# First token tiles turned one by one, W1 units begun on half of them, gate weights loaded as rows, and engine orders written out as a table

## The chip, the cores and the metric

The kernel runs on one core of one Trainium2 chip. A core has a matrix engine (PE), a vector engine (DVE), a scalar or activation engine (ACT), a general engine (POOL), a sequencer that mostly issues transfers (SP), and 16 DMA engines that all queues share. The engines run on their own instruction lists and meet at semaphores. The metric is the time of one execution in microseconds (us), and a version is judged by the median of several runs. The kernel before takes 154.9 us (three runs, 154.64 to 155.01).

## The reference

Two branches read the same 2048 tokens of width 512 and are mixed by a gate per token.

```
g = sigmoid((x * gate_w).sum(-1))                       # one number per token
# branch A: linear attention, 32 heads of 16
q, k, v = split(x @ wqkv)                               # 512 -> 3*512
pq, pk  = q @ w_phi, k @ w_phi                          # per head, 16x16
phi_q = concat(softmax(pq), softmax(-pq)); phi_k the same # 32 features a head
kv = phi_k^T v ; z = sum over tokens of phi_k
a  = ((phi_q kv) / (phi_q z + 1e-6)) @ wo
# branch B: dense layer with ReLU
b  = relu(x @ w1) @ w2                                  # 512 -> 1376 -> 512
out = g * a + (1 - g) * b                               # bf16
```

## The kernel before, in words

Tokens are cut into 16 tiles of 128, and into 4 chunks of 512 for the dense branch. The program is a graph of named tasks: each is one instruction, or a run of matmuls, with an engine, the tasks it depends on, and an assumed length and landing delay. A planner (`schedule`, lines 95 to 121) places the tasks with these assumed lengths, shakes its priorities 200 times, and keeps the order of each engine that gives its shortest plan. `emit` (line 133) then writes every engine's instructions in that order, with a semaphore wait wherever a dependency crosses engines. On the chip each engine follows its list strictly: an instruction that waits holds up all that stand behind it.

The names that the prediction uses:

- `x0a`, `x0b`: the first 512 tokens, loaded as two pieces of two tiles (256 KB each), one on SP's queue and one on ACT's. `xt..` turns them with PE against an identity (line 343; the identity is DVE's `ident`), four 128-column matmuls a bank, and `xe..` moves them from PSUM to `XT` (ACT line 355, DVE line 358). `x1`, `x2`, `x3` are the other three chunks, turned by DMA from SP (line 278); `x1` waits for `w1b1`.
- `w1a`, `w1b0`, `w1b1`, `w1c`: columns 0 to 255, 256 to 767 and 768 on of W1. `gw` puts the 512 gate weights as one more column into W1, element by element. `wka`, `wkb`: the K weights; `wv`: the V weights; `wphi`: the 16x16 head matrices, made block-diagonal by DVE (`wbd`).
- `h{c}_{k}` (line 398): unit k of W1 on chunk c, four matmuls of 512 columns, followed by `rl` (ReLU on ACT, line 413). Unit 10 carries the gate's column too: `gr` clips it, `g1`, `g2` take it through DRAM into one number per partition, `ge`, `gp`, `go` make the gate factors.
- `wt`, `we` (lines 329, 334, 336): K weights turned by PE and moved out. `f1_j`, `fe1_j` (line 373): W_phi folded into them, so that `pr_k..` gives pk directly. `f0_j` does the same for Q, turned by DMA (`wqT`).
- `pr_` (line 469): projections, two tiles a job (one in the last two jobs of a kind). `ev_` (ACT) copies them out, `mx_`, `mn_` (DVE) find the extremes of each head, `t1_`, `t2_` (POOL, line 510) subtract them, `ex_` (ACT) is the exponential, `sm_`, `rc_` (DVE) sum and invert, `nm_` (POOL) scales.
- `v{m}`, `ve{m}` (line 449): values of tile m. `kv{m}` (line 533) accumulates kv and z. `tq` turns phi_q by DMA, `nd{m}_{half}` (line 576) multiplies by kv, `rd`, `o` (DVE) divide, `to` turns the result by DMA.
- `b{m}` (line 597): W2 on tile m, eleven matmuls into one of three banks; `a{m}` (line 603) adds WO's product to the same bank; `oe{m}` (ACT, line 648) empties it; `st{m}` stores. The next user of a bank is `b{m+3}`.
- `warm` (line 260): eight matmuls on zeros while the first loads fly.

The order of the loads on each queue is fixed by hand:

```
load("x0a", "sp", ...); load("x0b", "act", ...); load("w1a", "sp", ...); load("wka", "act", ...)
load("wkb", "sp", ...); load("w1b0", "act", ...); load("w1b1", "sp", ...); load("wv", "act", ...)
load("w1c", "sp", ...); load("wphi", "pool", ...); load("gw", "pool", ...)
```

Of the kernel before, what the change touches and what calls it, by code (L numbers as in the profile page):

```python
# [6 lines left out]
ACT = mybir.ActivationFunctionType  # L7
# [6 lines left out]
ENGINES = ("sp", "pool", "act", "dve", "pe")  # L14

# [20 lines left out]
class _Graph:  # L36
# [28 lines left out]
    @staticmethod  # L65
    def lag(d, u):
        return 0.0 if u in d.behind or d.eng == u.eng == "pe" else d.lat

    @staticmethod
    def place(tasks, before, after, lag, key):  # L70

        left = {t: len(before[t]) for t in tasks}
        ready = {e: [] for e in ENGINES}
        for t in tasks:
            if not left[t]:
                ready[t.eng].append((0.0, t))
        free = dict.fromkeys(ENGINES, 0.0)
        order = {e: [] for e in ENGINES}
        start, end = {}, {}
        for _ in tasks:  # L80
            at, e = min((max(free[e], min(r for r, _ in ready[e])), e) for e in ENGINES if ready[e])
            pick = max((x for x in ready[e] if x[0] <= at), key=lambda x: key[x[1]])
            ready[e].remove(pick)
            t = pick[1]
            order[e].append(t)
            start[t], end[t] = at, at + t.dur
            free[e] = end[t]
            for u in after[t]:
                left[u] -= 1
                if not left[u]:  # L90
                    ready[u.eng].append((max(end[d] + lag(d, u) for d in before[u]), u))
        return order, start, end, max(end[t] + t.lat for t in tasks)

    def schedule(self, rounds=24, shakes=200):


        tasks = list(self.tasks.values())
        before = {t: list(dict.fromkeys(t.deps + t.ahead)) for t in tasks}
        after = {t: [] for t in tasks}
        for t in tasks:  # L100
            for d in before[t]:
                after[d].append(t)
        key = {}
        for t in reversed(tasks):
            key[t] = t.dur + t.lat + max((key[u] for u in after[t]), default=0.0)
        for t in tasks:
            key[t] += t.boost
        best = None
        rng = random.Random(1)
        for n in range(1 + shakes):  # L110
            if n:
                much = rng.choice((0.5, 1.0, 2.0, 4.0))
                at, wide = (rng.uniform(0.0, best[0]), rng.uniform(5.0, 40.0)) if n % 3 else (0.0, 1e9)
                key = {t: k + (much * rng.random() if abs(best[3][t] - at) < wide else 0.0) for t, k in best[2].items()}
            for _ in range(rounds if n == 0 else 3):
                order, start, end, span = self.place(tasks, before, after, self.lag, key)
                if best is None or span < best[0] + (1e-9 if n else -1e-9):
                    best = (span, order, key, start)
                key = {t: end[t] + t.lat for t in tasks}
                _, _, back, _ = self.place(tasks[::-1], after, before, lambda u, d: self.lag(d, u), key)  # L120
                key = {t: back[t] + 0.02 * t.boost for t in tasks}
        return best[1]
# [27 lines left out]
def bass_gated_mix__linear_kernel_hedgehog__dense_activation_relu__prompt_kernel(  # L150
# [33 lines left out]
    NWARM = 8  # L184
    RL = 400.0
    FE = "dve"
    SP0 = -1

    with ExitStack() as es:
# [35 lines left out]
        ROWM = sb("ROWM", [P, GH], I32)  # L225
        GB = sb("GB", [P, P], FP32)
# [55 lines left out]
        def chunk(c):  # L282
            return slice(c * 512, (c + 1) * 512)

        w1r = B_w1.rearrange("(j p) n -> p j n", p=P)
        x0r = x2[chunk(0), :].rearrange("(m p) d -> p m d", p=P)
        wkr = A_wqkv[:, D:2 * D].rearrange("(j p) n -> p j n", p=P)
        load("x0a", "sp", XN[:, 0:2, :], x0r[:, 0:2, :], dur=0.5, lat=3.7)
        load("x0b", "act", XN[:, 2:4, :], x0r[:, 2:4, :], dur=0.5, lat=3.7)
        load("w1a", "sp", W1[:, :, 0:256], w1r[:, :, 0:256], dur=0.5, lat=5.5)  # L290
        load("wka", "act", WK[:, 0:2, :], wkr[:, 0:2, :], dur=0.5, lat=5.0)
        load("wkb", "sp", WK[:, 2:4, :], wkr[:, 2:4, :], dur=0.5, lat=5.8)
        load("w1b0", "act", W1[:, 0:2, 256:768], w1r[:, 0:2, 256:768], dur=0.5, lat=8.0)
        load("w1b1", "sp", W1[:, 2:4, 256:768], w1r[:, 2:4, 256:768], dur=0.5, lat=8.0)
        load("wv", "act", WV[:, :, :], A_wqkv[:, 2 * D:3 * D].rearrange("(j p) n -> p j n", p=P), dur=0.5, lat=11.1)
        load("w1c", "sp", W1[:, :, 768:DFF], w1r[:, :, 768:DFF], dur=0.5, lat=10.4)
        load("wphi", "pool", WPS[:, :, :], A_w_phi.rearrange("(g hl) r c -> (hl r) g c", g=ND), dur=0.9, lat=5.7)
        load("gw", "pool", W1[:, :, DFF:DFF + 1], gate_w.rearrange("(j p o) -> p j o", p=P, o=1), dur=0.8, lat=8.0,
             allow_slow_non_contiguous=True)
        g.follow("iota_r", "iota_i")  # L300
        g.follow("iota_i", "wphi")
        load_t("x1", XT[:, :, chunk(1)], x2[chunk(1), :], ("w1b1",), 2.6, 2.3)
# [35 lines left out]
        XB, WB, FB = (0, 1, 6, 7), (2, 6, 7, 0), (1, 2, 6, 7)  # L338

        def pe_xt(q, p, hf):  # L340
            for n in range(4):
                j, m = 2 * p + n // 2, 2 * hf + n % 2
                last = q.matmul(PS[:, XB[2 * hf + p], n * P:(n + 1) * P], XN[:, m, j * P:(j + 1) * P], IDN[:, :],  # L343
                                start=True, stop=True)
            return last

        for hf, ld in enumerate(("x0a", "x0b")):
            half = slice(hf * 256, (hf + 1) * 256)
            for p in range(2):
                add(f"xt{p}{hf}", "pe", lambda q, p=p, hf=hf: pe_xt(q, p, hf), (ld, "ident"), dur=0.32,  # L350
                    boost=9000.0 - 10 * (ND * hf + p))
                o3 = XT[:, 2 * p:2 * p + 2, half]
                i3 = PS[:, XB[2 * hf + p], :].rearrange("p (j t) -> p j t", j=2)
                if p == 0:
                    add(f"xe{p}{hf}", "act", lambda q, o=o3, i=i3: q.activation(o, i, ACT.Copy), (f"xt{p}{hf}",),  # L355
                        dur=0.6, boost=9000.0)
                else:
                    add(f"xe{p}{hf}", "dve", lambda q, o=o3, i=i3: q.tensor_copy(o, i), (f"xt{p}{hf}",), dur=0.69,  # L358
                        boost=9000.0)
        for i in range(ND):  # L360
            add(f"wt{i}", "pe", lambda q, i=i: pe_turn(q, WB[i], [WK[:, j, i * P:(i + 1) * P] for j in range(ND)]),
                ("wka", "wkb", "ident",
                *((f"xe{XB.index(WB[i]) % 2}{XB.index(WB[i]) // 2}",) if WB[i] in XB else ())), dur=0.28, boost=1900.0)
            evict(f"we{i}", ("act", "dve")[i % 2], WT[:, ND + i, :], WB[i], (f"wt{i}",), boost=1900.0)
        x0 = [f"xe{p}{hf}" for p in range(2) for hf in range(2)]
# [11 lines left out]
        for j in range(ND):  # L377
            b = FB[j]
            war = ["xe10"] if j == 0 else [f"we{j - 1}"]
            add(f"f1_{j}", "pe", lambda q, j=j, b=b: pe_fold(q, 1, j, b), (*wkt, *wbd, *war), dur=0.24,  # L380
                boost=1800.0)
            evict(f"fe1_{j}", ("dve", "act")[j % 2], WP[:, 1, j, :], b, (f"f1_{j}",), boost=1800.0)
# [9 lines left out]
        freed = {b: () for b in HB}  # L392
        w1of = {k: (("w1a",) if k < 2 else ("w1b0", "w1b1") if k < 6 else ("w1c",)) for k in range(KT)}
# [7 lines left out]

        prev = None
        for n, (kind, a, k) in enumerate(units):
            b = HB[n % len(HB)]
            if kind == "h":
                rows = P if k < KT - 1 else KREM
                deps = [*xof[a], *w1of[k], prev, *freed[b]]
                if k == KT - 1:
                    deps.append("gw")
                add(f"h{a}_{k}", "pe", lambda q, a=a, k=k, b=b: pe_h(q, a, k, b), deps, dur=0.87,  # L410
                    boost=8000.0 if n < 2 else 0.0)
# [41 lines left out]
        for m in range(NT):  # L453
            def add(*a, boost=20.0 * (len(widths) * 2 - m // 2 - VLAG), **how):
                return g.add(*a, boost=boost, **how)

            add(f"v{m}", "pe", lambda q, m=m: pe_v(q, m), (*xof[m // 4], "wv", f"ve{m - 1}" if m else "fe1_1"), dur=0.87)
            add(f"ve{m}", "act", lambda q, m=m: q.activation(  # L458
                ap(VS, NT * NG * GZ, m * NG * GZ, [[GZ, NG], [1, GV]]), psap(2 * 512, [[GV, NG], [1, GV]]), ACT.Copy),
                (f"v{m}",), dur=0.6)  # L460
# [14 lines left out]
        for jn, (kind, tiles) in enumerate(jobs):  # L475
# [15 lines left out]
            def old(x, J2=two):  # L491
# [4 lines left out]
                 *([f"ev_{before}"] if before else ["fe1_0", "we3"])], dur=0.87 * w)  # L496
# [16 lines left out]
            if jn == NF - 2:  # L513
                war += [f"xt{p}{hf}" for p in range(2) for hf in range(2)]
# [197 lines left out]
```

## Time and profile before

| what | value |
|---|---|
| median of three runs | 154.9 us |
| the profiled execution | 155.05 us |
| its span in the profile | 153.5 us |
| PE busy | 148.2 us (97%) |
| POOL, DVE, ACT busy | 111.1, 114.2, 93.8 us |
| HBM read, written | 4.94 MB, 2.11 MB |
| first product of real data (line 398) | starts at 7.22 us |
| last product of PE | ends at 150.70 us |

The span runs from the first to the last instruction of the profiled execution; some 1.5 us of its time lie outside. Positions in the text, such as "at 7.22", are us from the start of the span. The chain of waits lists, in order of time, the pieces of work that led to the end, each with its start and its length. In the list of instructions a matmul's length includes its way through the array, so that the step from one to the next is shorter than its length.

### The profile page before, as it was taken

What the parts mean: (1) busy time and instruction counts of PE and PEld (TensorE: products, weight loads), DVE (VectorE), ACT (ScalarE), POOL (GpSimd) and SP (SyncE); (2) the same over time, 40 slices, a digit from 0 to 9 for tenths busy, and PEclk for the clock granted to TensorE, in tenths of its full rate; (3) what the DMA queues carried; (4) which work ended last, traced back from release to release, by engine and by line L of the source; (5) the groups of instructions that cost most, each with busy time, mean ns of one, the idle gap of its engine ahead of it and who ended that gap; (6) DMA issues with size and microseconds to landing.
All of it is one profiled execution on the core that took longest, in us unless ns stands there. A gap on an engine that the chain in (4) does not pass through costs nothing.

```text
span 153.5 us, 2500 instructions
## 1 busy us (share of the span) xinstructions
PE 148.2 (97%) x951; PEld 75.0 (49%) x951; DVE 114.2 (74%) x169; ACT 93.8 (61%) x127; POOL 111.1 (72%) x73
## 2 busy tenths in 40 slices
PE   6799999999999999999999999999999999999992
PEld 2565444554545544545454455444544444455471
DVE  3443668999986999489959969989889797773401
ACT  2366689869598959699789725586083612610331
POOL 7000396999999999999999999999895549260000
PEclk9999999999999999999999999999999999999999
DMA  4999999501000000000000050755869358696421
GB/s 139 261 351 240 134 221 334 156 1 1 6 0 0 0 5 0 2 0 0 1 4 0 10 127 7 138 127 138 193 162 169 102 137 205 152 145 154 117 86 36
DMA packets 43715, 15.59 MB, mean 102 GB/s; under 512 B 36548, under 2 KB 43700, under 8 KB 43704
## 3 DMA queue, kind: packets, MB, share of 16 engines
q1 hardware_dynamic: 39992, 12.08, 37.0%
q10 hardware_dynamic: 3648, 3.34, 6.7%
q0 software_dynamic: 64, 0.02, 0.5%
q8 instruction: 7, 0.11, 0.4%
q14 instruction: 4, 0.03, 0.1%
HBM read 4.94 MB, written 2.11 MB: 46 GB/s over the span
## 4 chain that ended last, share of the span: by engine, by line
PE 96%; DVE 1%; ACT 0%; issue 0%
PE PS L398 25%; PE PS L597 23%; PE PS L469 18%; PE PS L449 9%; PE PS L603 8%; PE PS L533 3%; PE PS L576 3%; PE PS L260 2%; PE PS L618 2%; PE PS L373 1%; PE PS L343 1%; PE PS L329 1%; PE PS L629 1%; DVE XT L358 0%; ACT OSB L648 0%
## 5 line engine op out<-in xcount | busy, mean ns | idle before, releaser
L519 DVE TENSOR_REDUCE ZB<-FT 128x128 f32<-128x2048 bf16 (+1 forms) x18 | 36.6, 2040 | 8.8 <-ACT FT L517 8.8
L398 PE MATMUL PS<-XT,W 128*128 128x512 bf16 (+1 forms) x176 | 41.4, 380 | 0.9 <-DVE XT L358 0.8
L510 POOL TENSOR_TENSOR TS<-MN,PB 128x1024 bf16<-128x1024 bf16 (+1 forms) x18 | 31.1, 1725 | 15.3 <-DVE MN L503 15.3
L597 PE MATMUL PS<-W,HT 128*128 128x512 bf16 (+1 forms) x165 | 38.1, 380 | 0.3 <-ACT OSB L648 0.3
L517 ACT ACTIVATE FT<-TS 128x2048 bf16<-128x2048 bf16 (+1 forms) x18 | 30.9, 1720 | 7.8 <-POOL TS L510 7.1
L510 POOL TENSOR_TENSOR TS<-PB,MX 128x1024 bf16<-128x1024 bf16 (+1 forms) x18 | 30.9, 1722 | 1.9 <-DVE MX L501 1.9
L469 PE MATMUL PS<-WP,XT 128*128 128x512 bf16 x128 | 30.6, 379 | 0.0
L526 POOL TENSOR_TENSOR FT<-FT,SC 128x2048 bf16<-128x2048 bf16 (+1 forms) x9 | 29.6, 3289 | 0.0
L413 ACT ACTIVATE HT<-PS 128x512 bf16<-128x512 f32 (+1 forms) x44 | 25.7, 598 | 6.0 <-PE PS L398 5.9
L398 PEld LDWEIGHTS PS<-XT,W 128*128 128x128 bf16 (+1 forms) x176 | 17.1, 100 | 19.8 <-ACT XT L355 1.0
L648 ACT ACTIVATE OSB<-PS,OMG 128x512 bf16<-128x512 f32 x15 | 10.3, 687 | 26.6 <-PE PS L603 26.1
L597 PEld LDWEIGHTS PS<-W,HT 128*128 128x128 bf16 (+1 forms) x165 | 15.4, 98 | 17.3 <-ACT OSB L648 0.4
L503 DVE TENSOR_REDUCE MN<-PB 128x64 bf16<-128x1024 bf16 (+1 forms) x18 | 19.3, 1074 | 3.5 <-ACT PB L497 3.4
L497 ACT ACTIVATE PB<-PS 128x1024 bf16<-128x1024 f32 (+1 forms) x18 | 16.7, 927 | 8.4 <-PE PS L469 8.1
L501 DVE TENSOR_REDUCE MX<-PB 128x64 bf16<-128x1024 bf16 (+1 forms) x18 | 19.4, 1077 | 2.2 <-ACT PB L497 2.2
L469 PEld LDWEIGHTS PS<-WP,XT 128*128 128x128 bf16 x128 | 12.1, 98 | 13.7
L449 PE MATMUL PS<-WV,XT 128*128 128x512 bf16 x64 | 16.4, 380 | 0.0
L549 POOL TENSOR_TENSOR FT<-FT,SR 128x1024 bf16<-128x1024 bf16 (+1 forms) x9 | 15.6, 1738 | 0.5
L603 PE MATMUL PS<-WO,OT 128*128 128x512 bf16 x60 | 15.1, 379 | 0.0
L584 DVE SCALAR_TENSOR_TENSOR OTM<-PS,EG,RD 128x256 bf16<-128x256 f32 x32 | 13.7, 466 | 0.0
L582 DVE RECIPROCAL RD<-PS 128x16 f32<-128x16 f32 x32 | 6.4, 229 | 7.2 <-PE PS L576 7.2
L458 ACT ACTIVATE VS<-PS 128x512 bf16<-128x512 f32 x16 | 9.5, 597 | 1.9 <-PE PS L449 1.9
(53 smaller groups left out, 96.5 us busy)
## 6 DMA issues: line engine op xcount, KB each, us to landing
out_dram<-OSB ACTq DMA_DIRECT2D x15, 128.0 KB, 1.9
W<-in_B_w_dram SPq DMA_DIRECT2D x1, 1280.0 KB, 7.5
W<-in_B_w_dram SPq DMA_DIRECT2D x1, 608.0 KB, 10.1
W<-in_B_w_dram SPq DMA_DIRECT2D x2, 256.0 KB, 6.4
WV<-in_A_wqkv_dram ACTq DMA_DIRECT2D x1, 512.0 KB, 10.7
WO<-in_A_wo_dram SPq DMA_DIRECT2D x1, 512.0 KB, 7.6
FT<-in_A_x_dram SPq DMA_DIRECT2D x1, 256.0 KB, 3.2
FT<-in_A_x_dram ACTq DMA_DIRECT2D x1, 256.0 KB, 3.5
```

What stands on the lines that cost most here:

```text
L398: last = q.matmul(PS[0:m, b, :], W1[:, j, k * P:k * P + m], XT[:, j, chunk(c)], start=(j == 0), stop=(j == ND - 1))
L413: add(f"rl{a}_{k}", "act", lambda q, a=a, k=k, b=b, rows=rows: q.activation(HT[0:rows, k, chunk(a)], PS[0:rows, b, :], ACT.Relu), (prev,), ...
L449: last = q.matmul(PS[:, 2, :], XT[:, j, m * P:(m + 1) * P], WV[:, j, :], start=(j == 0), stop=(j == ND - 1))
L469: last = q.matmul(PS[:, n, :], XT[:, j, m * P:(m + 1) * P], WP[:, s, j, :], start=(j == 0), stop=(j == ND - 1))
L501: add(f"mx_{J}", "dve", lambda q, sl=sl, w=w, i=pbg: q.tensor_reduce(MX[:, sl, 0:w * H], i, AX.X, ALU.max), (f"ev_{J}", old("t1")), dur=0. ...
L503: add(f"mn_{J}", "dve", lambda q, sl=sl, w=w, i=pbg: q.tensor_reduce(MN[:, sl, 0:w * H], i, AX.X, ALU.min), (f"ev_{J}", old("t2")), dur=0. ...
L510: add(f"{tn}_{J}", "pool", lambda q, o3=o3, a3=a3, b3=b3: q.tensor_tensor(o3, a3, b3, ALU.subtract), (f"{'mx' if sg == 0 else 'mn'}_{J}", ...
L517: add(f"ex_{J}", "act", lambda q, fs=fs, ts=ts, w=w: q.activation(FT[:, fs, 0:w * F], TS[:, ts, 0:w * F], ACT.Exp), (f"t1_{J}", f"t2_{J}", ...
L519: add(f"sm_{J}", "dve", lambda q, fs=fs, sl=sl, w=w: q.tensor_reduce(ZB[:, sl, 0:2 * w * H], FT[:, fs, 0:w * F].rearrange("p (g d) -> p g ...
L526: add(f"nm_{J}", "pool", lambda q, f3=f3, sl=sl, w=w: q.tensor_tensor(f3, f3, SC[:, sl, 0:2 * w * H].unsqueeze(2).to_broadcast([P, 2 * w * ...
L597: last = q.matmul(PS[:, ab, :], HT[0:r, k, m * P:(m + 1) * P], W2[0:r, k, :], start=(k == 0), stop=False)
L603: last = q.matmul(PS[:, ab, :], OT[:, m % NOT, t, :], WO[:, t, :], start=False, stop=(t == ND - 1))
```

## The change

What it does, part by part:

- The first 512 tokens come as four loads `x00` to `x03` of one tile each, two on SP's queue and two on ACT's. Each tile is turned on its own (`xt0` to `xt3`) into two half-filled banks, and moved out by two instructions of 256 columns, one on ACT (`xe{m}0`), one on DVE (`xe{m}1`).
- Units 0 and 1 of W1 on chunk 0 are split: `hh0`, `hh1` use the first 256 tokens, `h0_0`, `h0_1` the other 256.
- The loads are ordered anew: W1's first two column ranges in halves on both queues, then K weights as one load on SP, `w1c` on ACT behind `xe30`, V weights on SP. `x1` waits for `w1c` instead of `w1b1`.
- The gate weights are loaded as four rows of 128 (`GWR`), turned by one small matmul (`gt`) and copied into W1's extra column by DVE (`gv`).
- Four warm matmuls instead of eight; other PSUM banks at the start; Q's fold (`f0`) allowed after the whole of chunk 2.
- The planner is gone. The order of every engine is a written table.

```
-    def schedule(self, rounds=24, shakes=200):
...
+    def schedule(self):
+        order = {e: [self.tasks[n] for n in ORDER[e].split()] for e in ENGINES}
...
+ORDER = {
+    "sp": (
+        "x00 x01 w1a0 w1b0 wk wv x1 x2 g1_0 wqT x3 g2_0 g1_1 g2_1 w2a w2b tq0 wo tq1 g1_2 g1_3 g2_2 to0 tq2 tq3 "
...
+    "pool": (
+        "iota_c iota_r iota_i wphi gw t1_k0 t2_k0 t1_k1 t2_k1 ones nm_k0 t1_k3 t2_k3 t1_k2 t2_k2 t2_k4 t1_k4 "
+        "nm_k1 nm_k2 t2_k6 t2_k5 t1_k5 nm_k3 t1_k6 nm_k4 t2_k7 t1_k8 t1_k7 t2_k8 t2_q0 nm_k5 t1_q0 nm_k6 t1_q1 "
+        "ra_q0 t2_q1 nm_q0 nm_k7 nm_k8 t2_q2 t1_q2 ra_q1 nm_q1 t2_q3 t1_q3 ra_q2 nm_q2 t2_q4 t1_q4 ra_q3 nm_q3 "
...
+    "act": (
+        "x02 x03 w1a1 w1b1 xe00 xe10 xe20 xe30 w1c rl0_0 rl0_1 rl0_2 we2 we0 fe1_1 fe1_3 rl0_4 rl0_3 ev_k0 rl0_6 "
...
+        "rl3_5 ve14 ex_q1 rl3_7 ve15 ev_q4 rl3_6 rl3_8 rl3_9 ev_q5 ex_q2 ge2 oe0 gp2 st0 ex_q3 ev_q6 ge3 oe1 "
+        "ev_q7 ex_q4 oe2 oe3 ex_q5 ev_q8 st1 oe4 oe5 ex_q6 st3 st2 oe7 ex_q7 st5 st4 oe6 st7 oe9 ex_q8 st9 st6 "
+        "oe8 gp3 st8 oe10 oe11 oe12 st12 st10 oe13 oe14 st11 st14 st13 oe15_0 st15_0 "
+    ),
+    "dve": (
+        "zero ident shift xe01 xe11 xe21 blk xe31 wbd3 wbd0 wbd1 wbd2 we3 we1 gv fe1_0 fe1_2 mx_k0 mn_k0 mx_k1 "
+        "mn_k1 sm_k0 rc_k0 gr0 mx_k3 mx_k2 gr1 mn_k3 mx_k4 mn_k2 mn_k4 sm_k1 rc_k1 sm_k2 rc_k2 mn_k5 gr2 mn_k6 "
...
+    "pe": (
+        "warm xt0 xt1 xt2 xt3 hh0 hh1 h0_0 h0_1 h0_2 h0_3 wt3 wt2 wt1 wt0 h0_4 gt f1_0 f1_1 f1_2 f1_3 h0_5 pr_k0 "
+        "h0_6 h0_7 pr_k1 h0_8 v0 h0_9 pr_k2 h0_10 v1 pr_k3 h1_10 v2 h1_0 pr_k4 kv0 kv1 h1_1 h1_2 h1_3 v3 h1_4 "
...
+        "v11 h3_2 h3_3 pr_q2 kv10 v12 kv11 h3_4 h3_5 pr_q3 h3_6 kv12 v13 h3_7 kv13 v14 pr_q4 h3_8 v15 b0 kv14 "
+        "kv15 pr_q5 nd0_0 nd0_1 h3_9 nd1_0 nd1_1 b1 pr_q6 a0 b2 nd2_0 nd2_1 b3 nd3_1 a1 pr_q7 nd3_0 b4 nd4_1 "
+        "nd5_0 nd4_0 pr_q8 a2 nd5_1 a3 b5 nd7_0 nd6_0 nd6_1 b6 a4 nd7_1 a5 b7 nd8_1 nd8_0 b8 a7 a6 nd9_0 nd9_1 "
+        "b10 nd10_1 nd10_0 nd11_0 b9 a9 a8 nd11_1 b12 nd12_0 nd12_1 nd13_0 b11 nd14_1 nd14_0 a10 nd13_1 a11 b13 "
+        "nd15_1 nd15_0 a12 b14 a13 a14 b15 a15_0 a15_1 "
...
-    NWARM = 8
+    NWARM = 4
-    SP0 = -1
+    SP0 = -2
...
+        for n, lat in enumerate((2.7, 3.0, 3.4, 3.3)):
+            load(f"x0{n}", qs[n // 2], XN[:, n, :], x0r[:, n, :], dur=0.5, lat=lat)
+        for name, c0, c1, lat in (("w1a", 0, 256, 3.6), ("w1b", 256, 768, 4.6)):
+            for n in range(2):
+                load(f"{name}{n}", qs[n], W1[:, 2 * n:2 * n + 2, c0:c1], w1r[:, 2 * n:2 * n + 2, c0:c1], dur=0.5, lat=lat)
+        load("wk", "sp", WK, wkr, dur=0.5, lat=5.6)
+        load("w1c", "act", W1[:, :, 768:DFF], w1r[:, :, 768:DFF], dur=0.5, lat=3.2)
+        load("wv", "sp", WV[:, :, :], wvr, dur=0.5, lat=8.3)
+        load("wphi", "pool", WPS[:, :, :], A_w_phi.rearrange("(g hl) r c -> (hl r) g c", g=ND), dur=0.9, lat=6.2)
+        load("gw", "pool", GWR[0:ND, :], gate_w.rearrange("(j p) -> j p", p=P), dur=0.8, lat=4.5)
-        load_t("x1", XT[:, :, chunk(1)], x2[chunk(1), :], ("w1b1",), 2.6, 2.3)
+        load_t("x1", XT[:, :, chunk(1)], x2[chunk(1), :], ("w1c",), 2.6, 2.3)
...
+        def pe_xt(q, m):
+            for j in range(ND):
+                last = q.matmul(PS[:, XB[m][j // 2], (j % 2) * P:(j % 2 + 1) * P], XN[:, m, j * P:(j + 1) * P],
+                                IDN[:, :], start=True, stop=True)
+            return last
+        for m in range(4):
+            add(f"xt{m}", "pe", lambda q, m=m: pe_xt(q, m),
+                (f"x0{m}", "ident", *(("xe00", "xe01") if m == 3 else ())), dur=0.4, boost=9000.0 - 10 * m)
...
+        g.follow("xe30", "w1c")
+        add("gt", "pe", lambda q: q.matmul(PS[:, 2, 0:ND], GWR[0:ND, :], IDN[0:ND, 0:ND], start=True, stop=True),
+            ("gw", "ident", "xe20"), dur=0.06, boost=1500.0)
+        add("gv", "dve", lambda q: q.tensor_copy(
+            ap(W1, ND * W1C, DFF, [[W1C, ND], [1, 1]]), psap(2 * 512, [[1, ND], [1, 1]])), ("gt",), dur=0.15, boost=1500.0)
...
+        def pe_h_half(q, k, b):
+            for j in range(ND):
+                last = q.matmul(PS[:, b, 0:256], W1[:, j, k * P:(k + 1) * P], XT[:, j, 0:256],
+                                start=(j == 0), stop=(j == ND - 1))
+            return last
+        for k in range(2):
+            add(f"hh{k}", "pe", lambda q, k=k: pe_h_half(q, k, HB[k]), (*x0[0:4], "w1a0", "w1a1", prev), dur=0.44, boost=8500.0)
```

## The prediction

> **What bounds the kernel now.** I read the page's first part, then the chain of waits in order of time, then the loads, then busy time by stretch.
>
> ```profile
> span 153.5 us, 2500 instructions
> PE 148.2 (97%) x951; PEld 75.0 (49%) x951; DVE 114.2 (74%) x169; ACT 93.8 (61%) x127; POOL 111.1 (72%) x73
> ```
>
> PE is the bound; a change that leaves its work as it is can only remove idle PE time. The chain shows where that is:
>
> ```profile
> 1.19 3.60 PE PS L260 x8
> 4.79 1.61 PE PS L343 x16
> 6.40 0.02 issue
> 6.43 0.70 DVE XT L358
> 7.13 0.09 issue
> 7.22 1.89 PE PS L398 x8
> 9.11 0.89 PE PS L329 x16
> 10.00 0.10 issue
> 10.09 1.02 PE PS L398 x4
> 11.12 0.89 PE PS L373 x16
> 12.01 1.73 PE PS L398 x8
> 13.74 1.73 PE PS L469 x8
> ...
> 99.81 0.88 PE PS L603 x4
> 100.69 0.02 issue
> 100.71 0.70 ACT OSB L648
> 101.40 0.05 issue
> 101.45 2.55 PE PS L597 x11
> ```
>
> Product work starts at 7.22. From 13.74 to the last matmul at 150.70 PE stops once: 0.77 us (0.02 + 0.70 + 0.05) at 100.69, where b3 needs the bank that a0 has just filled and waits for oe0 to empty it. So two prizes: the start, and 0.77 us. What holds the start is loads and pace:
>
> ```profile
> q0 software_dynamic: 64, 0.02, 0.5%
> DMA to landing us min/median/max: 5.2/7.5/10.1
> 2.00:6.50 4.50, 4.39 (x23) 2.50 (x21) 1.13 (x4) 2.10 (x3) 1.94 (x4) 1.00 1.02 313
> 6.50:7.75 1.25, 0.53 (x3) 0.32 (x4) 1.09 (x4) 0.27 (x1) 0.00 (x0) 1.00 0.80 95
> 7.75:12.00 4.25, 4.16 (x44) 2.77 (x42) 1.89 (x6) 3.02 (x6) 0.00 (x0) 1.00 1.07 348
> ```
>
> The first line is POOL's queue (W_phi and the gate weights): 0.5% of 16 engines' span is 12.3 engine-us for 18 KB. The second is landing time of loads into W tiles within the first 13 us; the shortest, w1a, is issued at 1.26 and lands at 6.47. The last three are stretches (length, then busy time and count of PE, PEld, DVE, ACT, POOL, then clock, DMA share, GB/s): between 6.5 and 7.75 the rate falls from 313 to 95 GB/s while the DMA engines stay 80% busy, which is when the gate weights, 512 scattered elements, move (issued 2.31, 6.6 us to landing).
>
> **The change part by part.** The profiled execution took 155.05 us: 153.5 of span and 1.55 around it. The median of the three runs is 154.9, so sums made from the profile are lowered by 0.15.
>
> *Work.* Matmuls: the same products. hh0, hh1 and the rests of h0_0, h0_1 are 16 of 256 columns for 8 of 512; the 20 of L618 with 256 columns step at 0.11 us (22 in 2.41), half of 0.216, so nothing is added. gt is one tiny matmul (0.06). Four warm matmuls of 0.43 go; they lay before the first data.
>
> *First tokens.* Four 128 KB loads, issued as now at 0.74 and 0.5 us later on each queue. All 512 KB land as now at 4.25 (x0b: 0.75 + 3.5). x00 should land near 3.2: half of x0a's 256 KB left out at 313/2 GB/s is 0.8 off its 0.74 + 3.2; ends 2.9 and 3.94. xt0, 4 matmuls at the cold step of 0.107, is done by 3.9. ACT is not ready: its table load (2.88, 1.28 long) follows its fourth load, as it does in the changed order, so xe00 starts at 4.2; a half eviction costs near the 0.47 of the last tile's halves (0.60 is the 512-column one). xe00 ends at 4.67, and xt3, which reuses its bank, runs 4.75 to 5.2. xe10 ends by 5.1.
>
> *First units.* hh0 needs those and w1a, now two 128 KB pieces with 768 KB moved in all instead of the 1 MB that went by before 6.47: 256 KB at 313 GB/s is 0.84 less, 5.6; counted on from x0b, 4.25 + 0.84 = 5.1. I take 5.4, hh0 at 5.45; ends 5.2 (PE free) and 6.5 (w1a no earlier than now). PE's pace: L343 steps at 0.107 and L329, the same shape, at 0.056; the step changes at about 6.15, 4.95 us after the first matmul (the clock column says 1.00 throughout and does not show it). hh0 to h0_1, 1.73 at full pace, lose half of 0.70: they end at 7.53.
>
> *W1's next columns and the gate weights.* w1b now goes ahead of wk: 1.31 MB instead of 1.83 MB before it is complete. It landed at 9.96 (2.30 + 7.66); 0.5 MB at 348 GB/s is 1.5 less, and the dip, 1.25 x (1 - 95/313) = 0.87, goes with the 2-byte elements (four rows of 256 B). 7.6 at most; from x0b's 4.25 on, 0.79 MB at 348 GB/s give 6.5; PE wants it at 7.53 for h0_2. No wait taken, 0.1 possible. h0_3 ends at 9.26.
>
> *wk.* SP's fifth load, now beside w1c, which ACT issues only after xe30 (about 5.8, moving from 6.8). Near 6.6 all of wk is left; half of 348 GB/s gives 512 KB in 2.8 us: 9.4. Ends 8.7 (w1c late) and 12.1 (the whole first batch, WV's 2.35 + 10.7, less 0.87). wt starts at 9.45, h0_4 and all after it queued behind.
>
> *To the first projection.* wt 0.89, h0_4 0.86, gt 0.06; f1 waits for we1 (wt3's eviction starts at 9.87, two DVE casts of 0.69: 11.16, which h0_4 covers to 11.2): 11.26 to 12.15. h0_5 to 13.01; fe1_2, second of two casts from 11.68, ends at 12.98: pr_k0 at 13.08. Now it starts at 13.74 with one unit fewer done, so like for like at 14.60: **gain 1.52**.
>
> *Queues moved past.* SP issues x1's transpose after w1c (about 11.5, now 9.97): landings go from 14.9 to 16.8 and, for x2, from 18.9 to 21; pr_k2 wants x1 at 20.8, pr_k4 x2 at 28.6. g1_0 stands ahead of wqT and x3 and waits for gr0 near 27: x3 lands at about 35.5, pr_k6 wants it near 44, w2 near 86. All covered, by 4 us or more. On POOL iota_c ahead puts W_phi 0.2 later; it landed at 7.2, and wbd is wanted at 11.2. ones (0.69) moves from 3.26 to behind t2_k1, where POOL ends it at 25.5, before rc_k0 at 26.25.
>
> *The written-out order.* b2 (2.38) and nd2 (0.26) now stand between a0 and b3, against the 0.94 that b3 needed (nd2, right behind a0, starts at 100.51, b3 at 101.45): **0.77 gone**. What is tight next: b4, b5, b7, b12 and b13 have one a (b4: a one-tile pr) and one nd, 0.99, between filling and reuse; ACT must take the eviction within 0.05. Also kv0 (nm_k0: POOL from 26.3, 3.68 long, ends at 29.98; PE is there at 30.3) and kv15 right behind nm_k8. I charge 0.30 for these; ends 0 and 0.77, one stall like today's.
>
> Sum: 155.05 - 1.52 - 0.77 + 0.30 = 153.06, less 0.15: **152.9**.
>
> **The rivals.**
>
> *The pace doubles later.* Today PE runs without a gap from 1.19 until it doubles; then it has gaps near 3.0 and 3.7 us, some 0.6 in all. If the 4.95 us must be unbroken they start again at hh0 and end at 10.4: 2.48 lost, the four half units end at 11.38, pr_k0 starts at 15.01, 0.41 later than like for like: 155.05 + 0.41 - 0.77 + 0.30 - 0.15 = 154.84, no change. For it: fewer warm matmuls. Against it: PE is still busy four fifths of the 3 us before 6.15 (four xt of 0.43, 0.70 of hh0). The Trainium skill, TensorE: Matmul & The Clock Gate, Part 1, says full pace comes after one busy window of about 3.4 us of a free-running monitor; a missed window would by that be made good 3.4 us after 6.15, for which I estimate 154.4. The trace allows that rule (4.95 us from a cold start hold one whole window), but what share of a window must be busy neither says.
>
> *wk lands last.* PE's order is fixed, so everything stands behind wt. If wk is served after w1c and wv (12.1), wt starts at 12.15, pr_k0 at 15.78, 1.18 late: **155.6**, slower. It decides from a landing at 11.9. For: wk gains a competitor on the other queue, and lands now at 8.4 with less ahead of it. Against: wv is behind wk on the same queue.
>
> *The transfers hide the split.* w1a's last piece lands at 6.47 as now, hh0 at 6.52, already at full pace: pr_k0 at 13.61, gain 0.99, **153.4**.
>
> **How the numbers follow.** Forecast 0.60 (own range 152.3 to 153.4: wt near 8.9, or 0.77 of new waits), hidden split 0.15, late pace 0.14, late wk 0.11. A measurement tells 0.3%, 0.46 us, from no change. Faster: the first two, 0.75. Same: 0.14. Slower: 0.11. The range runs from 152.3 to 154.9 (late pace); late wk is left out.
>
> **What would show it.** The first W1 unit near 5.45 instead of 7.22; L329's successor near 9.45; the first WP product near 13.1; no 95 GB/s stretch; the idle time before b3 gone and less than 0.3 us of PE waits after 16 us. It is wrong if the first 128-column steps are still 0.107 after 7 us, if wt waits beyond 10, or if PE waits for ACT at several of the b's named.

## The result, and the profile after

The changed kernel takes 159.87 us (median of six runs, 158.68 to 162.32) against 154.85 for the kernel before (six runs, 154.64 to 155.3). The ratio is 1.0308, 95% interval 1.0238 to 1.0377: slower by 3%, where 152.9 was forecast. A ratio here leaves out runs more than 1.5% above the fastest of the same kernel, which a median and a range do not.

The profiled execution took 160.96 us with a span of 158.8; 153.5 was the span before. The six times lie in two groups, three from 158.68 to 158.9 and three from 160.84 on, and the profiled one is of the longer group. From its page, in the same order as before (the clock row has 40 slices of 4 us):

```profile
span 158.8 us, 2511 instructions
...
PE 150.1 (95%) x956; PEld 75.6 (48%) x956; DVE 121.1 (76%) x172; ACT 93.2 (59%) x129; POOL 111.0 (70%) x73
...
PEclk9999999999999999999997799999999999999999
...
q0 software_dynamic: 64, 0.02, 0.1%
```

DVE has 6.9 us more of busy time than before, though it has only three more instructions. The granted clock dips once, in the middle. The gate weights no longer hold the DMA engines: POOL's queue is down from 0.5% to 0.1%. The chain of waits, in order of time, shows the three places that matter:

```profile
1.68 5.58 DMA W<-in_B_w_dram
7.26 0.14 issue
7.40 1.87 PE PS L408 x8
9.27 1.53 PE PS L414 x8
10.79 1.73 PE PS L402 x8
12.52 0.89 PE PS L330 x16
13.41 0.86 PE PS L402 x4
14.28 0.11 PE PS L365
14.38 1.00 PE PS L377 x16
15.38 0.86 PE PS L402 x4
16.24 1.84 PE PS L495 x8
...
70.72 5.40 DVE MK L319
76.12 2.20 DVE ZB L545
78.32 2.25 DVE MX L527 x2
80.57 0.87 DVE SC L549
81.44 0.07 issue
81.51 3.68 POOL FT L552
85.19 0.05 issue
85.24 0.43 PE PS L559 x8
...
103.75 0.86 PE PS L629 x4
104.62 2.38 PE PS L623 x11
106.99 0.26 PE PS L602 x8
107.25 2.38 PE PS L623 x11
```

- Start: `hh0` begins at 7.40, not 5.45, because a piece of w1a lands at 7.26. The first WP product starts at 16.24; like for like, before had 14.60. That is 1.64 lost.
- Middle: the chain leaves PE for a DVE instruction of 5.40 us, line 319. It is `mk`, which makes a mask of 128x4 numbers. Behind it on DVE stand the sum, the extremes and `rc_k6`, and `nm_k6` on POOL waits for that; `kv12` on PE waits for `nm_k6`.
- End: behind `a0` (103.75) come `b2`, `nd2` and, at 107.25, `b3`, each at once. The 0.77 us stall is gone.

PE's two longest waits (us in total, times, longest), and then three stretches of 3.41 us (length, busy time and count of PE, PEld, DVE, ACT, POOL, granted clock, DMA share, GB/s):

```profile
PE PS L559 <- POOL FT L552: 2.7, 1, 2.7
PE PS L408 <- DMA W<-in_B_w_dram: 1.9, 1, 1.9
```

```profile
7.06:10.48 3.42, 3.08 (x15) 2.24 (x16) 0.77 (x4) 0.32 (x1) 0.00 (x0) 1.00 1.09 382
...
82.16:85.57 3.41, 0.71 (x11) 0.34 (x10) 3.41 (x5) 3.10 (x4) 3.41 (x2) 1.00 0.00 0
85.57:88.98 3.41, 3.41 (x14) 1.22 (x12) 3.41 (x6) 1.09 (x2) 2.50 (x3) 0.50 0.00 0
```

The wait for `nm_k6` costs 2.70. It leaves PE busy for only 0.71 of 3.41 us, and in the next 3.41 us the granted clock is 0.50: PE works all the time at half pace and loses another 1.71. The span's difference comes out: 1.64 + 2.70 + 1.71 - 0.77 = 5.28, against 158.8 - 153.5 = 5.3. Outside the span lie 2.2 us instead of 1.55, which no view of the profile explains.

What happened to `mk` is seen beside POOL. The two mask instructions (durations in ns, then the start), after and before:

```profile
L317 DVE TENSOR_SCALAR ROWM<-ROWS x1: 1211/1211/1211, 54.4 to 54.4; 128x4 int32<-128x4 int32 x1
L319 DVE TENSOR_TENSOR MK<-ROWM,COLH x1: 5403/5403/5403, 70.7 to 70.7; 128x4 f32<-128x4 int32 x1
```

```profile
L316 DVE TENSOR_SCALAR ROWM<-ROWS x1: 164/164/164, 1.5 to 1.5; 128x4 int32<-128x4 int32 x1
L318 DVE TENSOR_TENSOR MK<-ROWM,COLH x1: 156/156/156, 3.6 to 3.6; 128x4 f32<-128x4 int32 x1
```

And POOL's instructions in the changed kernel while `mk` ran, from its timeline (start, length, form, then idle time before):

```profile
69.55 2.93 POOL L536 TENSOR_TENSOR TS<-MN,PB 128x512 bf16<-128x512 bf16 x2
72.42 3.68 POOL L552 TENSOR_TENSOR FT<-FT,SC 128x2048 bf16<-128x2048 bf16 x1
79.52 1.91 POOL L536 TENSOR_TENSOR TS<-PB,MX 128x1024 bf16<-128x1024 bf16 x1 [3.42 <-DVE MX L527]
```

The same instructions, `row4` and `mk`, take 7 and 35 times as long in the middle as at the start. `mk` begins at 70.72, while POOL works, and ends at 76.12, 0.02 us after POOL's `nm_k5` (72.42 + 3.68 = 76.10). It lasts until POOL has nothing left to run: POOL's next instruction needs `mx`, which stands behind `mk`.

### The profile page after: what moved, and what is told of

Its sections match the earlier page's. It is cut to its first block, busy times and chain, and to the rows that moved or that the text cites. A ratio compares the mean times of both kernels' runs of the same rounds, so it can differ in the third digit from the quotient of the medians.

```text
span 158.8 us, 2511 instructions
## 1 busy us (share of the span) xinstructions
PE 150.1 (95%) x956; PEld 75.6 (48%) x956; DVE 121.1 (76%) x172; ACT 93.2 (59%) x129; POOL 111.0 (70%) x73
## 4 chain that ended last, share of the span: by engine, by line
PE 79%; DVE 12%; DMA 4%; POOL 2%; issue 1%; ACTq 1%
PE PS L623 22%; PE PS L402 19%; PE PS L495 13%; PE PS L629 8%; PE PS L475 6%; DMA W<-in_B_w_dram 4%; DVE MK L319 3%; DVE ZB L545 3%; PE PS L602 3%; POOL FT L552 2%; DVE MX L527 2%; PE PS L559 2%; DVE WP L337 2%; PE PS L644 2%; PE PS L408 1%; DVE SC L549 1%
## 5 line engine op out<-in xcount | busy, mean ns | idle before, releaser
L439 ACT ACTIVATE HT<-PS 128x512 bf16<-128x512 f32 (+1 forms) x44 | 25.2, 599 | 13.1 <-PE PS L402 8.6
L402 PEld LDWEIGHTS PS<-XT,W 128*128 128x128 bf16 (+1 forms) x168 | 16.5, 102 | 17.8 <-issue 1.1
L475 PE MATMUL PS<-WV,XT 128*128 128x512 bf16 x64 | 17.2, 394 | 0.0
```

Of the source, the lines that this page charges most:

```text
L402: last = q.matmul(PS[0:m, b, :], W1[:, j, k * P:k * P + m], XT[:, j, chunk(c)], start=(j == 0), stop=(j == ND - 1))
L439: add(f"rl{a}_{k}", "act", lambda q, a=a, k=k, b=b, rows=rows: q.activation(HT[0:rows, k, chunk(a)], PS[0:rows, b, :], ACT.Relu), (prev,), ...
L475: last = q.matmul(PS[:, 2, :], XT[:, j, m * P:(m + 1) * P], WV[:, j, :], start=(j == 0), stop=(j == ND - 1))
```

## The experiments

The theory after this reading: the masks' new place costs the middle; the start lost its gain to the loads and to the pace. The rivals: the middle's loss comes from the rest of the written order, or from the late start carried on; `mk` is slow for its type, not for its operands. All kernels but two start from the changed one.

**The masks put back to the start**, without and with eight warm matmuls, and the eight warm matmuls alone:

```
-  "... xe21 blk xe31 wbd3 ..."  "mx_k5 sm_k3 row4 rc_k3 ..."  "mn_q0 gr3 mk sm_k6 ..."
+  "... xe21 blk xe31 row4 mk wbd3 ..."  "mx_k5 sm_k3 rc_k3 ..."  "mn_q0 gr3 sm_k6 ..."
```

> The changed kernel with its two tiny mask instructions on DVE, row4 and mk, moved back to the start of DVE's list (behind xe31, ahead of wbd3), where POOL is idle; nothing else is touched. Theory (port): a DVE instruction that reads two SBUF operands, or a tensor_scalar on int32, waits until POOL's running instruction ends; mk ran 5.40 us at 70.72 and ended 0.02 us after POOL's nm_k5. Moved, the two take 0.16 us each, PE's 2.70 us wait for nm_k6 goes, and with it the half-pace stretch after it (1.71 us): the span falls from 158.8 by 4.4 to about 154.4, the time to about 156.5. Rival (place): something else holds DVE at that point (its instruction fetch, the wait behind gr3); then sm_k6 is still late by about 5 us and the time stays near 160.

> The changed kernel with eight warm matmuls instead of four. Theory (pace): PE must be busy without a larger gap for its step to halve; with eight, PE is busy from 1.19 to about 6.4 and hh0 to h0_1, which cost 3.2 us at the slow step from 7.40, run at the full one: the first WP product starts 1.3 to 1.6 us earlier than 16.24, and the time falls by as much, to about 159 on the scale of 160.5, with the 5 us of mk still in it. Rival (loads): W1a's landing at 7.26 alone sets the start; the pace doubles at a random moment whatever PE did; the time stays within 0.5 of the changed kernel's.

> Both edits, masks early and eight warm matmuls. If both theories hold the losses add: span 158.8 - 4.4 - 1.5 = 152.9, time about 154.9, no faster than the kernel before, because W1a still lands near 7.3. If only the port theory holds: 156.5. If only the pace theory: 159.

| kernel | median, us | all runs, us | ratio to before |
|---|---|---|---|
| e1, masks early, 4 warm | 156.07 (10 runs) | 153.6 to 156.97 | 0.9991 [0.9959, 1.0022] |
| e2, masks late, 8 warm | 158.78 (4 runs) | 158.44 to 158.9 | 1.0257 [1.0233, 1.028] |
| e3, masks early, 8 warm | 154.6 (10 runs) | 153.92 to 155.78 | 0.9996 [0.9966, 1.0025] |

Moving two instructions is worth 159.87 - 156.07 = 3.8 us with four warm matmuls and 158.78 - 154.6 = 4.2 with eight; the trace had 2.70 + 1.71 = 4.4. The two parts of the trace are not two separate costs, though. In e2's profiled execution, 158.44 us, `mk` took 5.40 us and PE waited the same 2.70 for POOL, but its steps stayed at full pace. It waited later instead, 0.34 us for POOL once more and 0.76 for ACT, a wait that e3 does not have:

```profile
PE PS L623 <- ACT HT L439: 0.8, 1, 0.8
```

That makes 3.80 us without any half pace. Its three other executions, with a mean granted clock of 0.989 as in the changed kernel's profile, took 158.75 to 158.9; in e4 below, two executions at 0.997 and 1.0 took 158.51 and 158.61, two at 0.988 and 0.989 took 158.65 and 158.76. So the work that `mk` held up on DVE and POOL sets most of the loss, and in these executions the half pace adds less than 0.5 us of its own to it.

In e1's timeline of DVE the sum follows the gate's clip at once, and PE waits for nothing after 16 us:

```profile
67.25 0.70 DVE L443 TENSOR_SCALAR GROW<-PS 1x512 f32<-1x512 f32 x1
67.98 2.29 DVE L545 TENSOR_REDUCE ZB<-FT 128x128 f32<-128x2048 bf16 x1
```

So the rest of the order costs nothing there. With the masks early and four warm matmuls, e1's times fall into two groups, 153.6 to 154.83 (four runs) and 155.68 to 156.97 (six). The profiled run is the fastest. From its timeline of PE:

```profile
1.19 1.89 PE L261 MATMUL PS<-TS 128*128 128x512 bf16 x4 [1.19 <-DVE TS L257]
...
5.74 1.03 PE L408 MATMUL PS<-XT,W 128*128 128x256 bf16 x8 [0.52 <-ACT XT L354]
6.61 1.04 PE L414 MATMUL PS<-XT,W 128*128 128x256 bf16 x8
```

Here w1a landed at 5.60, the pace doubled at 4.77, and the first two half units took 0.87 together, not 1.7: the first WP product came at 13.50 and the span was 151.5. In the changed kernel's run the pace doubled only at 10.48. I take the slower group for runs with a late pace; none of them was profiled, so this is argued. With eight warm matmuls (e3) no two groups are to be seen, and the range shrinks from 3.4 to 1.9 us.

**The masks moved late in the kernel before**, at the places that they have in the changed one, nothing else touched:

```
+ for n, behind in (("row4", "sm_k3"), ("mk", "gr3")):
+     order["dve"].remove(g.tasks[n])
+     order["dve"].insert(order["dve"].index(g.tasks[behind]) + 1, g.tasks[n])
```

> The kernel before, unchanged but for row4 put behind sm_k3 and mk behind gr3 in DVE's list, where the changed kernel has them. Port theory: POOL runs without a gap there, so mk runs several us instead of 0.16, and the time goes from 154.9 to between 156.5 and 161. Rival (place, or another part of the change): the two cost 0.3 us of DVE and the time stays within 0.5 of 154.9.

Measured: 158.63 us (four runs, 158.51 to 158.76), ratio 1.0251 [1.023, 1.0272]. The move alone makes the kernel before as slow as the changed one with eight warm matmuls. `mk` on DVE, and POOL's instructions at its end, from the timelines:

```profile
73.20 7.71 DVE L318 TENSOR_TENSOR MK<-ROWM,COLH 128x4 f32<-128x4 int32 x1
```

```profile
78.95 1.94 POOL L510 TENSOR_TENSOR TS<-PB,MX 128x1024 bf16<-128x1024 bf16 x1
82.12 1.91 POOL L510 TENSOR_TENSOR TS<-MN,PB 128x1024 bf16<-128x1024 bf16 x1 [1.23 <-DVE MN L503]
```

It waited through four whole instructions of POOL, without a gap between them, until POOL ran dry at 80.89, and ended at 80.91. PE lost 2.2 us waiting, and the half pace followed here too, from 88.72 to 92.13.

**What in the operands does it.** From e3, two small multiplications behind `gr3` whose results nothing uses, one with an operand in PSUM, one with both in SBUF, all in floating point (one run):

```
+ add("onep", "dve", ... q.tensor_tensor(DM[0:KREM, 0, :], PS[0:KREM, b, 0:GH], MK[0:KREM, :], ALU.mult) ...)
+ add("twos", "dve", ... q.tensor_tensor(DM[:, 1, :], GB[:, 0:GH], MK[:, :], ALU.mult) ...)
```

> The same base with two extra tiny DVE multiplications of four columns, results unused, put behind gr3, where the change has mk: the first reads one operand from PSUM and one from SBUF, the second reads both from SBUF, in fp32 this time. Port theory: the first takes about 0.2 us, the second runs until POOL's instruction ends, 1 to 6 us, and the time rises by 2 to 5 us over the base's 154.6. Rival (type): integers made row4 and mk slow, so both take 0.2 us. Rival (place): the first is the slow one.

Measured: 159.04 us. DVE, and then POOL, from the timelines:

```profile
68.58 0.16 DVE L449 TENSOR_TENSOR DM<-PS,MK 96x4 f32<-96x4 f32 x1
68.66 5.32 DVE L451 TENSOR_TENSOR DM<-GB,MK 128x4 f32<-128x4 f32 x1
```

```profile
67.39 2.93 POOL L543 TENSOR_TENSOR TS<-MN,PB 128x512 bf16<-128x512 bf16 x2
70.28 3.68 POOL L559 TENSOR_TENSOR FT<-FT,SC 128x2048 bf16<-128x2048 bf16 x1
```

The first ran in 159 ns beside the busy POOL; the second took 5316 ns and ended with POOL's last instruction (70.28 + 3.68 = 73.96). Neither the place nor the integer type makes the wait: two SBUF operands do. The two differ in 32 partitions as well, which I do not think matters but did not separate.

**Why w1a lands late.** Three edits on e3, one run each; the loads of that kernel bring 183 GB/s between 3.5 and 5.5 us, against 336 before.

```
e5
-  for name, c0, c1, lat in (("w1a", 0, 256, 3.6), ("w1b", 256, 768, 4.6)):
+  load("w1a", "sp", W1[:, :, 0:256], w1r[:, :, 0:256], dur=0.5, lat=5.5)
...
e6
-  for n, lat in enumerate((2.7, 3.0, 3.4, 3.3)):
-      load(f"x0{n}", qs[n // 2], XN[:, n, :], x0r[:, n, :], dur=0.5, lat=lat)
+  for n in (0, 2):
+      load(f"x0{n}", qs[n // 2], XN[:, n:n + 2, :], x0r[:, n:n + 2, :], dur=0.5, lat=3.7)
e7
-  load("wphi", "pool", WPS[:, :, :], A_w_phi.rearrange(...), dur=0.9, lat=6.2)
+  load("wphi", "pool", WPS[:, :, :], A_w_phi.rearrange(...), ("x03",), dur=0.9, lat=6.2)
```

> Masks early, eight warm matmuls, and W1's first 256 columns as one load on SP again instead of two on both queues; ACT's third load is then w1b1. The question is why the changed order moves 137 to 264 GB/s between 3.5 and 5.5 us where the kernel before moves 312 to 356, so that w1a lands at 5.6 to 7.3 instead of 6.4. Theory (short rows): W1's 512-byte rows on both queues at once leave the DMA engines short; with one queue of them beside w1b1's 1 KB rows, as before, the rate between 3.5 and 5.5 is over 300 GB/s and w1a lands by 5.8. Rivals (more loads; W_phi): the rate stays under 270 and w1a lands after 6.2.

> The same base (masks early, eight warm matmuls), W1 in halves as in the change, but the first 512 tokens as two loads of 256 KB instead of four of 128 KB. Theory (more loads): each boundary between two loads leaves the DMA engines short of work; with two fewer the rate between 3.5 and 5.5 us is over 300 GB/s. Theory (short rows) and theory (W_phi): it stays under 270 GB/s.

> The same base, but POOL issues the load of W_phi (512 pieces of 32 bytes) only when x03 has landed, near 4.3. In the changed kernel W_phi's packets move from 4.0 to 5.3, in the kernel before from 5.7. Theory (W_phi): the low stretch moves to about 7 us and the rate between 3.5 and 5.5 is over 300 GB/s. Theories (short rows; more loads): it stays under 270 GB/s. Its time is not of use, since W_phi lands later.

The rates in that stretch (columns as above) in e5, e6 and e7, in this order:

```profile
3.50:5.50 2.00, 2.00 (x14) 1.21 (x12) 0.25 (x1) 0.25 (x1) 0.00 (x0) 1.00 0.89 224
```

```profile
3.50:5.50 2.00, 2.00 (x13) 1.22 (x11) 0.25 (x1) 0.36 (x2) 0.00 (x0) 1.00 1.06 304
```

```profile
3.50:5.50 2.00, 2.00 (x13) 1.21 (x11) 0.25 (x1) 0.74 (x2) 1.03 (x2) 1.00 0.81 192
```

With w1a in one load it landed even later (7.67), 155.72 us was the time, and 224 GB/s is within what kernels with four token loads show anyway (183 to 268): its cut is not the cause. W_phi out of the way changed the rate by 9 GB/s (155.35; W_phi itself, now landing at 11.06, held its fold instead): not the cause. With two token loads of 256 KB instead of four of 128 KB the rate was back at 304 GB/s, w1a's pieces landed by 5.19, and `hh0` began at 6.33 right behind the last `xt`: 154.31. The four loads are the cause. Part of that is issuing: each load takes 0.41 to 0.47 us of ACT's queue, and w1a1 went out at 1.27 instead of 1.68. Why the rate falls as well stays open.

**Two token loads, masks early, six and four warm matmuls** (e6 with `NWARM = 6` and `NWARM = 4`):

> The candidate: the changed kernel with masks early, the first 512 tokens as two loads of 256 KB, and six warm matmuls. Theory (loads and pace both needed): x0 lands at 3.9 and 4.3, W1a by 5.3, PE is busy from 1.19 on with gaps under 0.4 us, hh0 starts near 5.7 instead of 7.40; the pace doubles by 8 at the latest in every run, so that the times spread little; the first WP product near 13.3 against 14.6 like for like before, and the 0.77 us before b3 stay gone: 153.4, between 153.0 and 154.2. Rival (pace is luck): with gaps the times spread as widely as with four warm matmuls, up to 157.

> The same with four warm matmuls as in the change. PE then idles from 2.9 to 4.0 us. Theory (pace): in some of its runs the pace doubles one step later and the time is 1.5 to 2 us longer, so that the median is 153.4 to 155.5 and the spread over 2 us. Rival: the spread of the changed order came from its late W1a alone, and this one is as even as with six and 0 to 0.3 faster.

| kernel | median, us | all runs, us | ratio to before |
|---|---|---|---|
| e9, six warm | 153.9 (6 runs) | 153.58 to 155.3 | 0.9939 [0.992, 0.9958] |
| e10, four warm | 154.63 (12 runs) | 153.52 to 155.77 | 0.9989 [0.9963, 1.0016] |

e9 is faster than the kernel before by 0.6%, which is little, but its interval ends below 1; by the medians it is some 3.7% faster than the changed kernel. The rates of these two (318 and 305 GB/s) bear out e6. With four warm matmuls the loads are as early, but PE starts W1 at half pace, as e10's timeline of PE shows: the eight products of line 408 take 1.7 us up to the next line, where e1 needed 0.87.

```profile
5.74 1.92 PE L408 MATMUL PS<-XT,W 128*128 128x256 bf16 x8
7.44 1.35 PE L414 MATMUL PS<-XT,W 128*128 128x256 bf16 x8
```

e9's median lies in the range that was expected. Its profiled execution is its longest, 155.3, and not for its start: the first WP product starts at 13.89, 0.36 before e10's. Apart from the wait before its first matmul, PE waits twice in it:

```profile
PE PS L602 <- DMA PHQ<-FT: 1.3, 1, 1.3
PE PS L402 <- DMA W<-in_B_w_dram: 0.5, 1, 0.5
```

The second is `h0_2` waiting for w1b. The first is `nd` waiting for the DMA that turns a late tile of phi_q; it is issued at 131.87 and lands at 137.53. So the start is not all that spreads the times.

**The gate weights as four rows, in the kernel before**, its planned order kept as a table with `gt` and `gv` put in:

```
-  load("gw", "pool", W1[:, :, DFF:DFF + 1], gate_w.rearrange("(j p o) -> p j o", p=P, o=1), ...)
+  load("gw", "pool", GWR[0:ND, :], gate_w.rearrange("(j p) -> j p", p=P), ...)
```

> The kernel before with its planned order written out, and the gate weights alone loaded as four rows, turned by gt on PE behind f1_0 and copied by gv. Theory: the stretch of 45 to 168 GB/s near 7 us goes, W1b lands 0.9 us sooner, but h0_2 stands behind wt, so only its 0.1 to 0.25 us of waiting is gained, less 0.06 for gt: 154.6, no change that can be told. Rival (loads set the start): W1b sooner moves everything, 154.0 or less.

Measured: 154.62 us (10 runs), ratio 0.9983 [0.9968, 0.9998]. The stretch that had 95 GB/s before:

```profile
6.50:7.75 1.25, 1.25 (x6) 0.58 (x7) 0.00 (x0) 0.19 (x1) 0.00 (x0) 1.00 1.11 347
```

The dip is gone, and w1b1 lands at 9.24 instead of 9.96, but that wait was not the last at the start: 0.2% is within what a measurement tells from no change.

## Why the prediction was wrong

*The step that failed is "The written-out order".* It went through PE's new order in the b's, the kv's and the banks, and "Queues moved past" went through SP and POOL. DVE's list was not gone through. On it `row4` and `mk` moved from 1.5 and 3.6 us to 54.4 and 70.7, into stretches where POOL works without a gap. Priced by their own rows they cost 0.3 us and nothing visible; in the new place they cost 2.70 + 1.71, more than the range is wide (2.6). The charge for new waits was 0.30 with ends 0 and 0.77. Against the sum's span of 151.5 the profiled execution has 7.3 us more: these 4.41, and 3.16 at the start (below), less the 0.30 that was not needed. By e2 the 1.71 is no separate price: without the half pace the middle still lost 3.80. None of the rivals was this one; e4 shows it in the kernel before, and e8 which operands it takes. The two rows of e8 show one rule: a tensor_tensor of DVE that reads two SBUF operands is held while POOL works through its tensor_tensors, and one that reads one of them from PSUM is not. The Trainium skill, SBUF — State Buffer, "Who interferes with whom", states it: DVE and GpSimd share a pair of ports as an exclusive lock, and "A DVE instruction with two SBUF inputs contends with a GpSimd instruction that reads SBUF". The runs agree (159 against 5316 ns), but the wait lasts longer than the one instruction of POOL that runs when it begins. It should have made a rival with a chance. (`row4`, with one operand, was held too, for 1.05 us; no experiment is about it.)

*The half pace behind it* was not thought of in the middle of a kernel. The pace changes on a raster: from 10.48 to 85.57 are 22.0 times 3.413 us. After a stretch with PE busy 21% the next is at half pace; where the same wait fell across two stretches (e2, 55% and 66%), it was not. The Trainium skill, TensorE: Matmul & The Clock Gate, Part 1, speaks of a free-running window of about 3.4 us; the runs agree.

*First tokens: right in the first tile, wrong in what it does to the rest.* x00's tile was turned from 3.41 (a landing near 3.2 was forecast). "All 512 KB land as now" held in this execution: x03 was issued at 1.19 and landed 3.0 later, at 4.2. That w1a follows at 313 GB/s failed: behind the four loads the rate between 3.5 and 5.5 us was 203 GB/s.

*First units: w1a at 5.4 became 7.26*, outside the ends of 5.2 and 6.5; in e1 it was 5.60. So `hh0` came 1.95 us late. The doubling of the pace, set at 6.15 as in the run before, came at 10.48 and cost 1.54 instead of 0.35. Together 3.14, which is the way from the forecast 13.08 to 16.24 (3.16). The late pace had been a rival, for another reason than the true one: no unbroken stretch is needed, but a window that is busy enough (e1's, from 1.35 to 4.77, had gaps and 3.04 us of work), and when the windows fall changes from run to run. (In that rival 11.38 is the end of `h0_3`, not of the four half units; its sum holds.) The hidden split came true too, worse than stated.

*Right:* no 0.77 before `b3`; the gate weights' dip gone, and worth nothing by itself (e11), as the working had it off the path; wk (9.6, where 9.4 was forecast) in time for its user; no wait of PE after 16 us but the one that `mk` made, so b4 to b13 and kv0 cost nothing and the 0.30 was not needed; x1 to x3 covered behind SP's new order. *Luck:* w1b, "7.6 at most", landed at 8.57, and nothing waited for it only because `hh0` was late; in e1 and e9, with an earlier start, PE waited 0.24 and 0.50 us for it. And with the masks back and an early pace the sum seems to hold: e1's profiled span is 151.5, and 153.06 - 1.55 is 151.5 too. But its first WP product starts at 13.50, 0.42 later than the 13.08 of the sum, and the unneeded 0.30 makes up for most of that. It is also the best of ten runs, not the median; what lies outside the span is 0.55 more than counted.

## What to carry to other kernels

When orders are written anew, go through every engine's list, also that of the engine that is not the bound, and ask of each instruction that moves what runs beside it in its new place: a mask of 0.16 us can cost 4 us there, and cost nothing at the start. A price from a trace holds for the neighbours that it had. Cut first loads no smaller than needed, and keep the matrix engine busy until the real work comes: both kernels with two token loads and masks early brought the loads forward, but only the one with six warm matmuls was measurably faster.

## What the runs showed of the hardware

- A DVE instruction with two SBUF operands does not get in between two of POOL's instructions that follow without a gap: it waited through the rest of one and the whole of the next in the changed kernel, through four whole ones in e4 (7.71 us), until POOL had nothing to run. Beside a memset of POOL's, which reads nothing (before, from 3.26 to 3.95), the same `mk` took 0.16 us. `row4`, with one operand, waited only for the instruction that ran: it ended at 55.58, and POOL went on at 55.52.
- The clock of PE needs a window of 3.41 us that is busy enough. In the changed kernel's start, stretches of the raster with 2.13 and 1.83 us of busy time (62% and 54%) did not bring full pace; the next, with 3.08 (90%), did. In the middle, 0.71 us (21%) lost it. Other traces narrow this. In e3, where full pace came at 7.21, the stretch up to 3.80 had 2.61 us (76%) and did not bring it, the one from 3.80 had 2.75 (81%) and did. In e4, 1.25 us (37%) lost it; in e2, two stretches of 1.88 and 2.25 (55% and 66%) in a row kept it. So here the share that brings full pace lies between 76% and 81%, and the share below which it is lost between 37% and 55%.
- The raster's place differs from run to run: full pace came at 6.15 us in the profiled run before, at 10.48 after, at 4.77 in e1 and 4.21 in e11. With four warm matmuls the stretch up to 4.77 in e1 was busy for 3.04 of 3.41 us (89%) and brought it.
- Four token loads of 128 KB in place of two of 256 KB lowered the rate just behind them from 304 or more to 183 to 268 GB/s (e6, e9, e10 and before against the changed kernel, e1 and e3). Why is open, as is why some 2.1 us lie outside the span in the kernels with four such loads, but 1.9 to 2.0 in those with two and in e5, which has four and w1a in one piece, and 1.55 in the kernel before.
